# Attention, a gated feed-forward and a maxout feed-forward: which engine makes the low parts of the value weights

## The chip, the cores and the metric

The kernel runs on one core of a Trainium2 chip. The metric is device time in microseconds (us) of one execution, taken as the median over several runs. Five engines work side by side, each on its own instruction queue and in the order of that queue: PE (TensorE, matrix products), DVE (VectorE, elementwise work), ACT (ScalarE, activations and copies), POOL (GpSimd, elementwise work here), and SP (SyncE), which only issues DMAs. A wait between engines is a semaphore.

## The reference, cut to what matters

```python
scores = q @ k.T / sqrt(D)                 # B=4, H=8, S=576, D=64
# heads 0-3: local window of 32; heads 4-7: same position modulo 32; both causal
attn = softmax(where(mask, scores, -1e9))
x = (attn @ v) reshaped to 2304 x 512
g = x @ w_gate;  val = x @ w_val           # 512 x 1536 each
x = (silu(g) * val) @ w_out                # 1536 x 512
h = max(x @ w1, x @ w2, x @ w3)            # 512 x 768 each
return h @ w_out2                          # 768 x 512
```

The weights come in as 64-bit floats.

## The kernel before

Each matrix product in the feed-forwards is made from split numbers: an operand is a high part (rounded to the format `F32R`) and a low part (what the rounding left), and one product is three matmuls, high by high, high by low and low by high (`product`, lines 484 to 486). So every weight tile goes through these steps before PE can use it:

- `load` (L138) brings the 64-bit words of a 128x512 tile into SBUF by a DMA of SP.
- `convert` (L141 to L159) makes a 32-bit float from the two halves of each word: two ACT instructions (L151, L152), then four on DVE (L154, L156, L157, L158). The first three tiles have a step or two on POOL instead.
- `split_w` (L161 to L170) makes the high part by an ACT copy (L126), the low part by one subtraction, weight minus high part (L129), on the engine that `step_split` hands over. Value and output weights are then stored to DRAM by a DMA of SP (L170), since later columns of tokens read them back (`reload`, L723). Gate weights stay in SBUF.

There are 36 such tiles in the first feed-forward: a gate tile g, a value tile v and an output tile o for each of the 12 slices f of its inner dimension. Their order (L686 to L691) is g0, v0, g1, v1, o0, g2, v2, o1 and so on to g11, v11, o10, o11. `step_split` counts them in `n_split`; for each third one, from the first, it takes DVE for the low part, and POOL for the others. By the order above the DVE ones are g0 and v1 to v11, twelve in all; v0, the other gate tiles and all output tiles are POOL's.

The 2304 tokens stand in five columns c = 0 to 4 of some 480 tokens. Attention for column 0 comes first. Then loops run over c and, within it, over f: `emit_gate` (12 matmuls into ps_g, then Silu by ACT, L504), `emit_val` (12 matmuls into ps_v, then DVE multiplies by the gate, L511, ACT makes the high part hh, L126, and POOL the low part hl, L129), and one slice late `emit_out` (12 matmuls into ps_y). While c is 0, a `weight_step` stands ahead of the gate, the value and the end of each slice: it loads a tile, converts one and splits one. Attention of the next column is put between (`attention_steps`): block softmax on DVE, ACT and POOL (L294 to L304), its results split by ACT and DVE (L328, L329), and, for rows that aren't done on PE, elementwise products on POOL (L397, L419) that DVE sums (L400, L422). From column 1 on no weights of the first feed-forward are converted any more, but those of the second are, at a slower pace. After column 4 the second feed-forward runs.

The order in which each engine gets its instructions is not the order of the source: a planner lays them out when the kernel is built, by an estimate of when each would be ready. From then on each engine's queue is fixed.

Of the kernel before, what the change touches and what calls it, by code (L numbers as in the profile page):

```python
# [57 lines left out]
def tile_attention_swiglu_maxout(  # L58
# [11 lines left out]
    nc = tc.nc  # L70
# [29 lines left out]
    def f32(ap):  # L100
        return ap.bitcast(F32)
# [20 lines left out]
    def split(hi, lo, src, hi_eng, lo_eng):  # L122
        if hi_eng is nc.gpsimd:
            a = nc.gpsimd.tensor_scalar(hi, src, 1.0, 1.0, ALU.mult, ALU.mult)
        elif hi_eng is nc.scalar:
            a = nc.scalar.activation(hi, src, AF.Copy)  # L126
        else:
            a = nc.vector.tensor_copy(hi, src)
        return a.ins, lo_eng.tensor_tensor(lo, src, f32(hi), ALU.subtract).ins  # L129
# [31 lines left out]
    def split_w(key, lo_eng):  # L161
        name = f"{key[0]}{key[1]}"
        if key[0] == "g":
            wt[key] = tuple(wpool.tile([128, 512], F32R, name=f"w{p}_{name}", tag="w") for p in "hl")
        else:
            t = (wv_p if key[0] == "v" else wo_p).tile([128, 2, 512], F32R, name=f"w_{name}", tag="w")
            wt[key] = (t[:, 0], t[:, 1])
        split(*wt[key], cvt.pop(key), nc.scalar, lo_eng)
        if key[0] != "g":
            nc.sync.dma_start(wdr[key], f32(t))  # L170
# [515 lines left out]
    first = [("g", 0), ("v", 0)]  # L686
# [5 lines left out]
    n_load, n_cvt, n_split = [0], [0], [0]  # L692
# [17 lines left out]
    def step_split(eng):  # L710
        if n_split[0] < limit[0]:
            key = order[n_split[0]]
            split_w(key, nc.vector if n_split[0] < len(first) and n_split[0] % 3 == 0 else eng)
            n_split[0] += 1

    def weight_step():
        step_load(n_cvt[0] + AHEAD)
        step_cvt()
        step_split(nc.gpsimd)
# [6 lines left out]
    if True:  # L726
# [8 lines left out]
        for i in range(len(blocks) + lag):  # L735
# [5 lines left out]
            if i >= lag:  # L741
                blocks[i - lag].transpose(nc.vector if i % 3 == 2 else nc.scalar)
                blocks[i - lag].pv()
        step_split(nc.gpsimd)
        step_split(nc.gpsimd)
        step_load(n_cvt[0] + 2)
        step_cvt()
# [178 lines left out]
```

## Time and profile before

| | |
|---|---|
| median of 3 runs | 881.88 us (879.77 to 882.62) |
| the profiled execution's own time | 881.39 us |
| span of its instructions | 879.6 us |
| busy share of the span: PE, DVE, ACT, POOL | 93%, 63%, 44%, 43% |
| column 0 of the first feed-forward | from about 42 us to about 190 us |

The busy share is an average over stages. A DVE instruction that stands on its engine counts as busy also while it is held up, so busy time has to be laid beside what the same instruction takes at its shortest. In the views below, a start time is in us from the beginning of the span, the number after it is the duration, and "[0.92 <-DVE w_v L129]" says that the engine was idle for 0.92 us until that instruction of another engine ended.

### The profile page before, as it was taken

The page shows a single profiled execution, that of the slowest core. Times are in us where ns is not written, and L with a number is a line of the kernel's source. Part 1 is how long each engine was busy: PE and PEld are TensorE (multiplying, and loading weights), DVE is VectorE, ACT ScalarE, POOL GpSimd, SP SyncE. Part 2 cuts the span into 40 slices and gives each one's busy share as a digit, 9 for nine tenths or more (in the row PEclk, how much of TensorE's full clock was granted, in tenths as well). Part 3 has the DMA queues.
Part 4 walks back from the last instruction along what each step waited for, and adds up shares of the span by engine and source line. Part 5 has one row for each costly group of instructions (what it writes and reads, how often), then busy time and mean ns, then how long its engine had stood idle before and what let it go on. Part 6 is the DMA issues. An engine that isn't in the chain of part 4 may idle for free.

```text
span 879.6 us, 12559 instructions
## 1 busy us (share of the span) xinstructions
PE 820.3 (93%) x4376; PEld 731.7 (83%) x4376; DVE 555.9 (63%) x1097; ACT 384.0 (44%) x857; POOL 382.3 (43%) x301
## 2 busy tenths in 40 slices
PE   5789879898999989999998889999999999999997
PEld 5677658687788878999897779989999899989986
DVE  2988999967757598668768943433545254433441
ACT  4778586734445454364634233432335123422221
POOL 0443654474757676667596632430213021211110
PEclk9789789999999999999999989999999999999999
DMA  9868757896695759869676687578856476453601
GB/s 234 244 219 289 235 187 260 320 366 189 209 330 192 245 190 312 275 207 319 208 249 234 224 268 225 189 245 342 330 217 213 182 251 245 175 215 118 241 1 72
DMA packets 81774, 203.76 MB, mean 232 GB/s; under 512 B 9484, under 2 KB 50224, under 8 KB 78128
## 3 DMA queue, kind: packets, MB, share of 16 engines
q1 hardware_dynamic: 81712, 202.97, 68.1%
q8 instruction: 35, 0.57, 0.2%
q14 instruction: 27, 0.22, 0.1%
HBM read 161.26 MB, written 41.68 MB: 231 GB/s over the span
## 4 chain that ended last, share of the span: by engine, by line
PE 49%; DVE 10%; DMA 4%; ACT 4%; issue 3%; POOL 2%; SPq 0%; DVEq 0%; ACTq 0%; POOLq 0%
PE ps_a L585 13%; PE ps_z L658 8%; PE ps_c L585 6%; PE ps_b L585 3%; PE ps_v L484 2%; PE ps_g L484 2%; PE ps_v L485 2%; PE ps_v L486 2%; PE ps_g L486 2%; PE ps_g L485 2%; PE ps_y L484 2%; PE ps_y L486 2%; PE ps_y L485 2%; DVE w L156 2%; DMA w_v<-wvdr 1%
## 5 line engine op out<-in xcount | busy, mean ns | idle before, releaser
L129 POOL TENSOR_TENSOR hl<-t,hh 128x384 fp32r<-128x384 f32 x36 | 37.6, 1048 | 208.5 <-ACT hh L126 167.2
L484 PE MATMUL ps_g<-xh,wh_g 128*128 128x448 f32 (+1 forms) x240 | 94.4, 393 | 10.4 <-ACT ht L504 8.1
L129 POOL TENSOR_TENSOR hl<-ht,hh 128x448 fp32r<-128x448 f32 (+1 forms) x60 | 75.5, 1258 | 60.5 <-ACT hh L126 58.8
L419 POOL TENSOR_TENSOR pr<-stv,stsc 128x1088 f32<-128x1088 f32 (+17 forms) x44 | 75.2, 1710 | 58.1 <-DVE sto L422 35.9
L486 PE MATMUL ps_v<-xh,w_v 128*128 128x448 f32 (+1 forms) x240 | 91.5, 381 | 8.2 <-DVE w_v L129 8.2
L484 PE MATMUL ps_v<-xh,w_v 128*128 128x448 f32 (+1 forms) x240 | 92.4, 385 | 4.4 <-ACT w_v L126 2.4
L585 PE MATMUL ps_a<-yhT,wr 128*128 128x384 f32 x324 | 94.4, 338 | 0.6 <-ACT s L599 0.6
L486 PE MATMUL ps_g<-xh,wl_g 128*128 128x448 f32 (+1 forms) x240 | 92.7, 386 | 1.3 <-POOL wl_g L129 1.3
L485 PE MATMUL ps_g<-xl,wh_g 128*128 128x448 f32 (+1 forms) x240 | 92.4, 385 | 0.0
L485 PE MATMUL ps_v<-xl,w_v 128*128 128x448 f32 (+1 forms) x240 | 91.1, 379 | 0.0
L485 PE MATMUL ps_y<-hl,w_o 128*128 128x448 f32 (+1 forms) x240 | 89.2, 376 | 1.0 <-POOL hl L129 1.0
L397 POOL TENSOR_TENSOR pr<-stk,stq 128x1088 f32<-128x1088 f32 (+17 forms) x44 | 76.9, 1747 | 30.1 <-DVE stsc L400 23.2
L486 PE MATMUL ps_y<-hh,w_o 128*128 128x448 f32 (+1 forms) x240 | 86.4, 377 | 2.3 <-POOL w_o L129 2.3
L484 PE MATMUL ps_y<-hh,w_o 128*128 128x448 f32 (+1 forms) x240 | 86.2, 380 | 0.2 <-ACT w_o L126 0.2
L599 ACT ACTIVATE s<-ps_a 128x384 f32<-128x384 f32 x81 | 39.4, 490 | 98.4 <-PE ps_a L585 98.1
L126 ACT ACTIVATE hh<-ht 128x448 fp32r<-128x448 f32 (+1 forms) x60 | 35.2, 587 | 106.0 <-DVE ht L511 105.6
L658 PE MATMUL ps_z<-wo2t,hh 128*128 128x512 f32 x216 | 64.8, 392 | 0.9 <-ACT osb L667 0.7
L484 PEld LDWEIGHTS ps_g<-xh,wh_g 128*128 128x128 f32 x240 | 47.2, 197 | 19.1 <-ACT ht L504 10.5
L511 DVE TENSOR_TENSOR ht<-ps_v,ht 128x448 f32<-128x448 f32 (+1 forms) x60 | 37.8, 630 | 37.9 <-PE ps_v L486 26.6
L585 PEld LDWEIGHTS ps_a<-yhT,wr 128*128 128x128 f32 x324 | 59.7, 188 | 1.7 <-ACT s L599 1.1
L486 PEld LDWEIGHTS ps_v<-xh,w_v 128*128 128x128 f32 x240 | 46.1, 192 | 15.1 <-DVE w_v L129 10.3
L484 PEld LDWEIGHTS ps_v<-xh,w_v 128*128 128x128 f32 x240 | 46.2, 192 | 11.1 <-DVE ht L511 3.4
(134 smaller groups left out, 1971.5 us busy)
## 6 DMA issues: line engine op xcount, KB each, us to landing
wr<-wsdr SPq DMA_DIRECT2D x27, 1792.0 KB, 7.2
raw<-in_w_dram SPq DMA_DIRECT2D x60, 512.0 KB, 4.8
w_v<-wvdr SPq DMA_DIRECT2D x48, 512.0 KB, 5.0
w_o<-wodr SPq DMA_DIRECT2D x48, 512.0 KB, 4.9
wsdr<-whi SPq DMA_DIRECT2D x27, 256.0 KB, 3.3
wvdr<-w_v SPq DMA_DIRECT2D x12, 512.0 KB, 4.1
wodr<-w_o SPq DMA_DIRECT2D x12, 512.0 KB, 5.2
loct<-in_loc_dram SPq DMA_DIRECT2D x24, 192.0 KB, 6.5
```

Source lines behind the costliest of these rows:

```text
L126: a = nc.scalar.activation(hi, src, AF.Copy)
L129: return a.ins, lo_eng.tensor_tensor(lo, src, f32(hi), ALU.subtract).ins
L156: nc.vector.tensor_scalar(w, w, 3, 0x3FFFFFFF, ALU.logical_shift_left, ALU.bitwise_and)
L397: eng.tensor_tensor(pv, self.k[:, 0:i + 1, :], self.q[:, r:r + 1, :].to_broadcast([128, i + 1, D]), ALU.mult)
L419: eng.tensor_tensor(pv, self.v[:, :, 0:i + 1], self.sc[:, r:r + 1, 0:i + 1].to_broadcast([128, D, i + 1]), ALU.mult)
L484: nc.tensor.matmul(ps, wh, xh, start=first, stop=False)
L485: nc.tensor.matmul(ps, wh, xl, start=False, stop=False)
L486: nc.tensor.matmul(ps, wl, xh, start=False, stop=last)
L511: m = nc.vector.tensor_tensor(t, ps[:, :n], t, ALU.mult).ins
L585: nc.tensor.matmul(ps, wts[:, c, a, ks], y[k][b], start=first and k == q == 0, stop=k == 1 and q == 2, skip_group_check=True,)
L599: nc.scalar.activation(s, self.a, AF.Copy)
L658: nc.tensor.matmul(z[j], a[:, ts], w[:, f, b], start=f == q == 0, stop=f == NF2 - 1 and q == 2)
```

## The change

In `step_split` the low part of every tile is made by the engine handed over, which is POOL at each call. The twelve low parts g0 and v1 to v11 leave DVE for POOL. What is computed, its buffers and its DMAs are the same.

```diff
     def step_split(eng):
         if n_split[0] < limit[0]:
             key = order[n_split[0]]
-            split_w(key, nc.vector if n_split[0] < len(first) and n_split[0] % 3 == 0 else eng)
+            split_w(key, eng)
             n_split[0] += 1
```

## Rows read from the trace of the kernel before

**Rows 1.** The page, first part: busy time and share of each engine.
```profile
PE 820.3 (93%) x4376; PEld 731.7 (83%) x4376; DVE 555.9 (63%) x1097; ACT 384.0 (44%) x857; POOL 382.3 (43%) x301
```
**Rows 2.** Busy us by stretch: length, PE, PEld, DVE, ACT, POOL, clock, DMA, GB/s.
```profile
50.00:90.00 40.00, 36.77 (x188) 29.83 (x188) 36.60 (x72) 31.44 (x61) 17.04 (x12) 0.96 0.82 269
90.00:178.00 88.00, 73.75 (x372) 59.26 (x373) 87.67 (x156) 59.74 (x127) 47.29 (x33) 0.88 0.75 252
178.00:200.00 22.00, 20.53 (x103) 17.39 (x102) 14.80 (x32) 7.78 (x23) 16.43 (x9) 1.00 0.99 355
```
**Rows 3.** DVE groups, 26 to 185 us: count, busy us, mean ns, idle before, releaser.
```profile
L158 DVE CUSTOM_DVE_ANT_0 w<-w,q 128x1024 uint16<-128x1024 uint16 x36 | 34.4, 960 | 0.1
L129 DVE TENSOR_TENSOR w_v<-w,w_v 128x512 fp32r<-128x512 f32 x11 | 11.0, 996 | 2.6 <-ACT w_v L126 2.6
```
**Rows 4.** By tile or line: shortest, median and longest ns of one.
```profile
L129 DVE TENSOR_TENSOR w_v<-w,w_v x11: 676/682/2559, 45.4 to 174.6; 128x512 fp32r<-128x512 f32 x11
L129 POOL TENSOR_TENSOR wl_g<-w,wh_g x11: 1282/1306/1794, 45.7 to 167.5; 128x512 fp32r<-128x512 f32 x11
L158 DVE CUSTOM_DVE_ANT_0 w<-w,q x36: 670/682/1776, 31.1 to 177.5; 128x1024 uint16<-128x1024 uint16 x36
L511 DVE TENSOR_TENSOR ht<-ps_v,ht x12: 640/646/659, 52.1 to 179.3; 128x480 f32<-128x480 f32 x12
```
**Rows 5.** Timeline: POOL low parts, each with the DVE instruction beside it.
```profile
53.63 1.80 POOL L129 TENSOR_TENSOR w_o<-w,w_o 128x512 fp32r<-128x512 f32 x1 [4.94 <-ACT w_o L126]
54.22 1.77 DVE L158 CUSTOM_DVE_ANT_0 w<-w,q 128x1024 uint16<-128x1024 uint16 x1
...
65.11 1.34 POOL L129 TENSOR_TENSOR w_o<-w,w_o 128x512 fp32r<-128x512 f32 x1 [1.29 <-ACT w_o L126]
65.23 1.78 DVE L158 CUSTOM_DVE_ANT_0 w<-w,q 128x1024 uint16<-128x1024 uint16 x1
...
134.25 1.31 POOL L129 TENSOR_TENSOR wl_g<-w,wh_g 128x512 fp32r<-128x512 f32 x1 [0.17 <-ACT wh_g L126]
134.28 1.33 DVE L422 TENSOR_REDUCE sto<-pr 128x64 f32<-128x1152 f32 x1
...
175.41 1.36 POOL L129 TENSOR_TENSOR w_o<-w,w_o 128x512 fp32r<-128x512 f32 x1 [1.62 <-ACT w_o L126]
175.82 1.49 DVE L157 SCALAR_TENSOR_TENSOR w<-raw,w 128x512 int32<-128x512 int32 x1
```
**Rows 6.** A POOL group, 26 to 185 us, columns as in rows 3.
```profile
L129 POOL TENSOR_TENSOR wl_g<-w,wh_g 128x512 fp32r<-128x512 f32 x11 | 16.0, 1452 | 12.2 <-ACT wh_g L126 10.8 <-issue 1.4
```
**Rows 7.** PE's waits, 50 to 178 us: total, times, longest.
```profile
PE ps_v L486 <- DVE w_v L129: 8.2, 6, 2.9
PE ps_y L486 <- POOL w_o L129: 2.3, 1, 2.3
```
**Rows 8.** Timeline around the low part of v7.
```profile
121.77 0.62 ACT L126 ACTIVATE w_v<-w 128x512 fp32r<-128x512 f32 x1
126.95 2.66 DVE L156 TENSOR_SCALAR w<-w 128x512 int32<-128x512 int32 x1
129.52 0.68 DVE L129 TENSOR_TENSOR w_v<-w,w_v 128x512 fp32r<-128x512 f32 x1
130.26 0.73 PE L486 MATMUL ps_v<-xh,w_v 128*128 128x480 f32 x1 [2.93 <-DVE w_v L129]
```
**Rows 9.** Timeline at the end of the conversions and behind it.
```profile
174.59 0.68 DVE L129 TENSOR_TENSOR w_v<-w,w_v 128x512 fp32r<-128x512 f32 x1
175.32 0.49 PE L486 MATMUL ps_v<-xh,w_v 128*128 128x480 f32 x1 [0.92 <-DVE w_v L129]
179.05 0.39 DVE L329 TENSOR_TENSOR xl<-ps_a,xh 128x120 fp32r<-128x120 f32 x1
181.31 0.37 PE L486 MATMUL ps_g<-xh,wl_g 128*128 128x480 f32 x1
201.72 0.86 PE L309 MATMUL ps_a<-cst,sm 128*96 128x128 f32 x4 [2.38 <-POOL sm L304]
```

## The prediction

> **What bounds the kernel now.** The page's first part [rows 1] seems to settle it: PE is busy for 93% of the span, DVE for 63%, POOL for 43%. That is an average, and eleven of the twelve low parts start between 45.4 and 174.6 us [rows 4], so the second view is busy time by stretch [rows 2]. From 90 to 178 us DVE is busy 87.67 of 88 us, while PE is busy 73.75 and its clock was granted at 0.88, a mean of the two levels of 2.4 and 1.2 GHz. POOL is busy 47.29. Before that, from 50 to 90 us, DVE is busy 36.60 of 40. So while column 0 runs, DVE sets the pace with the conversions, PE waits for weights, and POOL has room. Behind 178 us DVE is at 14.80 of 22 and PE goes on.
>
> The third view says what DVE is busy with [rows 3, 4]. L158 takes 682 ns at the median, 670 at the shortest, but 960 on average and 1776 at the longest: it is held up. The timeline names by whom [rows 5]: at 65.11 POOL starts a low part that takes 1.34 us, L158 starts at 65.23 and ends some 0.55 us behind POOL's end, having taken 1.78. The hold is 1.78 - 0.68 = 1.09 us. It isn't so for all kinds: L511, which reads PSUM, takes 640 to 659 ns in all twelve cases [rows 4], and the sum L422, which reads one SBUF tensor, runs to its 1.33 us beside a POOL low part as if alone [rows 5]. The conversion steps and the low parts themselves are of the kind that is held.
>
> The fourth view is PE's waits in this stretch [rows 7]: the longest in total is on the DVE low parts, 8.2 us in 6 waits, as DVE reaches them late. For v7 ACT has made the high part at 122.39, and DVE does the low part at 129.52, behind an L156 that took 2.66 us beside a long POOL product [rows 8]; PE waited 2.93.
>
> **Removed from DVE.** Twelve subtractions, each 0.68 us at the median [rows 4], from an engine that is full: 12 x 0.68 = 8.2 us. Their mean of 996 ns [rows 3] is larger by holds; I don't count those as gain, since the next held kind in the queue takes the hold. DVE also idled 2.6 us ahead of eleven of them, for ACT's high part [rows 3]. I take 2.0 of it, as it counts only where what stands behind is ready.
>
> **Added to POOL.** Twelve subtractions of 1452 ns mean [rows 6], 1282 at the shortest [rows 4]: 17.4 us. POOL has 88 - 47.29 = 40.7 us free between 90 and 178 alone [rows 2], so their time as such is hidden. On POOL's queue hl, w_o's low parts, the softmax products L304 and the products L397 and L419 may stand behind them, each later by up to 1.5 us. hl has a slice of cover, as the output product comes one slice late. For w_o the cover has been gone once: 2.3 us of PE wait [rows 7]; once more would cost as much. SP stores a value tile when its low part is there, so the store, and the raw loads queued behind it, follow the low part; where that comes sooner, so do they. g0 is the first tile, before column 0's matmuls begin at about 42 us, and counts in the sums for DVE alone.
>
> **What twelve more POOL low parts cost DVE** is the price that decides, and no row shows it for v tiles in this place. I went through the 32 POOL low parts between 53 and 177 us (11 w_o, 11 hl, 10 wl_g), the first and last of which stand in rows 5, and took what the DVE instruction beside each lost against its shortest: 27.3 us, 0.85 each. The ends: the ten wl_g give 0.52, as some meet sums and PSUM readers; a full hold is 1.09 [rows 5]. A v low part will stand on POOL directly behind wl_g or hl, while DVE has conversions queued, so I take the mean: 12 x 0.85 = 10.2 us. DVE's sum is then 10.2 - 8.2 = +2.0, and with the idle time 10.2 - 8.2 - 2.0 = 0. Below nothing is in reach: 12 x 0.52 - 10.2 = -4.0. Above: 12 x 1.09 - 8.2 = +4.9.
>
> Rows 5 show a hold of 1.09 us from an operation of 1.34, and none on a sum or a PSUM reader. The Trainium skill, SBUF — State Buffer, section SBUF: two separate sides, speaks against this change: DVE and GpSimd share one pair of ports as an exclusive lock, held for a whole instruction, and a DVE instruction with two SBUF inputs, or in a mode of two ports, fully blocks behind GpSimd. The trace agrees in who is held, but not for the whole of POOL's recorded time; by the rule each move would cost the mean of 1.45 us, 12 x 1.45 - 8.2 = +9.2 us, an estimate; by the rows it is +2.0 before the idle time.
>
> **What PE makes of it.** The low part on POOL can start when ACT's high part and POOL's own queue allow, not 7 us later as for v7 [rows 8]. But PE is fed by the conversions, so its waits can't all turn into time. At the end of the stage PE waits 0.92 us for v11 at 175.32; the next thing from DVE is the last piece of column 1's input, xl, written 179.05 to 179.44 and read from 181.31 on [rows 9], so PE can run ahead there by 181.31 - 179.44 = 1.9 us before it meets the next limit. I take half of it, 1.0 us, as DVE's own order may shift.
>
> **The sum.** DVE 0, PE's lead -1.0: 881.39 - 1.0 = 880.4 us against the profiled execution (span 879.6 and 1.8 around it). That lies 0.5 below the median of the runs, 881.88; on the median's footing the forecast is 880.9. It is no change that can be measured: 0.3% of this kernel is 2.6 us, about what a measurement here can tell from none, so the bounds are 879.2 and 884.5.
>
> **Rivals.**
> Faster: the moved parts meet the cheap neighbours, as wl_g does. DVE's sum is -4.0, PE's lead the whole 1.9: -5.9 us, 876.0. For it speak PE's 8.2 us of waits [rows 7] and the clock of 0.88 [rows 2], which gives back time when waits go; against it that DVE, not PE, is full, and that behind the stage PE waits 2.38 us at 201.72 for a softmax product of POOL [rows 9], where a lead can be lost again.
> Slower: DVE meets a full hold each time, since POOL's operations now stand back to back (wl_g, v, hl) and each ends a turn in which DVE gets one instruction through. +4.9, no idle time won and no lead: 886.8. For it: the longest L158 [rows 4], and that DVE's queue between 90 and 178 us is mostly conversions. Against it: 0.85 on average includes such pairs already. It decides from 0.68 + (2.0 + 1.0 + 2.6) / 12 = 1.15 us per move if idle time and lead are won, from 0.90 if neither is.
> Nothing arrives: the low part has to queue on POOL behind hl, wl_g and the long products, and comes no sooner than from DVE. Then DVE's +2.0 stays alone: 883.9, still within the bounds. That the change doesn't act can't be: it only names another engine.
> The planner may also lay out other queues anew. What that moves isn't in the trace; I bound it on both sides by the mean of the six PE waits, 8.2 / 6 = 1.4 us.
>
> **How the numbers follow.** The forecast and the nothing-arrives case, both no change: 0.38. Faster: 0.33. Slower: 0.29, of which 0.05 for a hold as long as POOL's whole operation, 1.45 each [rows 6], 881.4 + 9.2 = 890.6. The range goes from 876.0 - 1.4 = 874.6 to 886.8 + 1.4 = 888.2, cut to 887.5, as both at their worst is unlikely.
>
> **What would show it.** In the changed trace DVE has no low part of a weight, POOL has 36. The mean of L154 to L158 rises: if the holds come to 0.85 each, their sum by some 10 us; if to 0.5, by 6; if to 1.1, by 13. PE's wait on DVE for v low parts is gone; what stands in its place (ACT's high parts, or POOL's low parts) tells whether lag or supply was the limit. The low part of v11 stands at 174.59 now [rows 9], and DVE's last conversions just behind it; they should end within 2 us of where they do. The prediction is wrong if that moves by more, or if PE's clock in this stretch rises clearly above 0.88.

## The result, and the profile after

The changed kernel is slower: 887.74 us median of 4 runs (886.65 to 888.91) against 880.90 (879.77 to 882.62) for the kernel before on the same chip. The ratio is 1.0077, 95% interval 1.0058 to 1.0096: +6.8 us, and just outside the range that was forecast (874.6 to 887.5). The profiled execution took 888.02 us, its span is 886.2.

The page's first part of the changed kernel says almost the same as [rows 1]: DVE has twelve instructions less and is busy 2 us longer, POOL twelve more and 14.5 us longer.

```profile
PE 819.2 (92%) x4376; PEld 727.5 (82%) x4376; DVE 558.0 (63%) x1085; ACT 384.1 (43%) x857; POOL 396.8 (45%) x313
```

Busy time by stretch of the changed kernel, columns as in [rows 2]: length, PE, PEld, DVE, ACT, POOL, clock, DMA share, GB/s.

```profile
50.00:90.00 40.00, 36.02 (x206) 28.50 (x205) 38.15 (x68) 31.34 (x63) 21.90 (x17) 0.96 0.76 247
90.00:178.00 88.00, 68.65 (x340) 53.84 (x339) 83.95 (x148) 58.20 (x122) 50.20 (x37) 0.90 0.73 240
```

From 90 to 178 us DVE is no longer full: 83.95 of 88 us, where it was 87.67. PE did less there, 68.65 us and 340 matmuls, where it was 73.75 and 372. So DVE was relieved in the stage that it had bounded, and the stage got longer all the same.

The groups of DVE's conversion steps, 26 to 185 us, and POOL's new one (columns as in [rows 3]), then the same POOL group as shortest, median and longest:

```profile
L158 DVE CUSTOM_DVE_ANT_0 w<-w,q 128x1024 uint16<-128x1024 uint16 x36 | 35.5, 987 | 0.2
L157 DVE SCALAR_TENSOR_TENSOR w<-raw,w 128x512 int32<-128x512 int32 x36 | 34.4, 957 | 0.3
L156 DVE TENSOR_SCALAR w<-w 128x512 int32<-128x512 int32 x36 | 26.0, 724 | 0.3
L154 DVE TENSOR_SCALAR w<-w 128x512 f32<-128x512 f32 x33 | 22.1, 668 | 5.0 <-ACT w L152 5.0
...
L129 POOL TENSOR_TENSOR w_v<-w,w_v 128x512 fp32r<-128x512 f32 x12 | 17.1, 1423 | 15.1 <-ACT w_v L126 13.7 <-issue 1.3
...
L129 POOL TENSOR_TENSOR w_v<-w,w_v x12: 1275/1454/1592, 36.6 to 174.5; 128x512 fp32r<-128x512 f32 x12
```

Before, L158 took 34.4 us [rows 3] and the other three:

```profile
L157 DVE SCALAR_TENSOR_TENSOR w<-raw,w 128x512 int32<-128x512 int32 x36 | 32.8, 917 | 0.1
L156 DVE TENSOR_SCALAR w<-w 128x512 int32<-128x512 int32 x36 | 21.7, 604 | 0.2
L154 DVE TENSOR_SCALAR w<-w 128x512 f32<-128x512 f32 x33 | 21.3, 646 | 1.2 <-ACT w L152 1.2
```

So the four conversion groups took 110.2 us together before; now 118.0. That is +7.8, or 0.65 for each of twelve new POOL operations. L154 waited 1.2 us for ACT's L152 before and waits 5.0 now: part of DVE's new room is a wait for another engine.

PE's waits of the changed kernel from 50 to 185 us (total, times, longest), and the longest of them in the timeline:

```profile
PE ps_g L484 <- ACT wh_g L126: 8.9, 4, 6.2
PE ps_v L484 <- DVE ht L511: 2.7, 2, 1.7
...
PE ps_v L486 <- POOL w_v L129: 1.3, 2, 0.8
...
127.45 0.77 PE L484 MATMUL ps_g<-xh,wh_g 128*128 128x480 f32 x1 [6.16 <-ACT wh_g L126]
```

The wait that the change is aimed at is nearly gone: 8.2 us on DVE's low parts [rows 7], 1.3 on POOL's. In its place PE waits 8.9 us for high parts of gate tiles (0.9 before), and one wait alone is 6.16. It is for the eighth gate tile, g7, and this is what stood around it on POOL, DVE and ACT:

```profile
120.15 2.46 POOL L419 TENSOR_TENSOR pr<-stv,stsc 128x1152 f32<-128x1152 f32 x1
120.61 2.28 DVE L154 TENSOR_SCALAR w<-w 128x512 f32<-128x512 f32 x1 [0.70 <-ACT w L152]
...
126.77 0.63 ACT L126 ACTIVATE wh_g<-w 128x512 fp32r<-128x512 f32 x1 [1.38 <-DVE w L158]
```

An L154 of that tile stood beside a long POOL product for 2.28 us, and ACT could make the high part only at 126.77. In the kernel before, ACT had started it at 118.55. The last conversion ends late too; here it is with PE's first gate matmul of column 1, in the changed kernel:

```profile
182.16 1.40 DVE L158 CUSTOM_DVE_ANT_0 w<-w,q 128x1024 uint16<-128x1024 uint16 x1
...
184.91 0.38 PE L484 MATMUL ps_g<-xh,wh_g 128*128 128x480 f32 x1
```

And the same three, g7's high part, the last conversion and the gate matmul, in the kernel before:

```profile
118.55 0.62 ACT L126 ACTIVATE wh_g<-w 128x512 fp32r<-128x512 f32 x1
...
177.52 0.69 DVE L158 CUSTOM_DVE_ANT_0 w<-w,q 128x1024 uint16<-128x1024 uint16 x1
...
179.36 0.37 PE L484 MATMUL ps_g<-xh,wh_g 128*128 128x480 f32 x1
```

The last conversion ends at 183.56, where it ended at 178.21 before, and PE's gate matmul starts at 184.91, where it was 179.36. So +5.4 us is there when column 0 ends, of the 6.6 by which the two profiled executions differ (888.02 - 881.39).

Two things changed at once: twelve operations went to another engine, and the planner, given other costs, laid out all queues anew. The experiments take them apart.

### The profile page after: what moved, and what is told of

It is laid out like the page before. It is cut to its first block, busy times and chain, and to the rows that moved or that the text cites. A ratio compares the mean times of both kernels' runs of the same rounds, so it can differ in the third digit from the quotient of the medians.

```text
span 886.2 us, 12557 instructions
## 1 busy us (share of the span) xinstructions
PE 819.2 (92%) x4376; PEld 727.5 (82%) x4376; DVE 558.0 (63%) x1085; ACT 384.1 (43%) x857; POOL 396.8 (45%) x313
## 4 chain that ended last, share of the span: by engine, by line
PE 45%; DVE 13%; issue 4%; DMA 3%; ACT 3%; POOL 3%; SPq 0%; DVEq 0%; ACTq 0%; POOLq 0%
PE ps_a L585 12%; PE ps_z L658 8%; PE ps_c L585 6%; PE ps_b L585 3%; DVE w L156 2%; PE ps_g L484 2%; PE ps_v L484 2%; PE ps_g L485 2%; PE ps_y L486 2%; PE ps_y L485 2%; PE ps_g L486 2%; PE ps_y L484 2%; PE ps_v L486 2%; PE ps_v L485 2%; DMA w_v<-wvdr 1%
## 5 line engine op out<-in xcount | busy, mean ns | idle before, releaser
L486 PE MATMUL ps_g<-xh,wl_g 128*128 128x448 f32 (+1 forms) x240 | 92.9, 387 | 2.2 <-POOL wl_g L129 2.2
L486 PE MATMUL ps_v<-xh,w_v 128*128 128x448 f32 (+1 forms) x240 | 90.9, 379 | 1.3 <-POOL w_v L129 1.3
L486 PE MATMUL ps_y<-hh,w_o 128*128 128x448 f32 (+1 forms) x240 | 87.2, 374 | 1.0 <-POOL w_o L129 1.0
L484 PEld LDWEIGHTS ps_g<-xh,wh_g 128*128 128x128 f32 x240 | 47.0, 196 | 29.0 <-ACT ht L504 12.2
L484 PEld LDWEIGHTS ps_v<-xh,w_v 128*128 128x128 f32 x240 | 46.0, 192 | 19.4 <-DVE ht L511 7.9
L158 DVE CUSTOM_DVE_ANT_0 w<-w,q 128x1024 uint16<-128x1024 uint16 x60 | 54.8, 914 | 0.8
```

The costliest lines, as they stand in the source:

```text
L158: nc.vector.tensor_tensor(w, w, q, ALU.add)
L484: nc.tensor.matmul(ps, wh, xh, start=first, stop=False)
L486: nc.tensor.matmul(ps, wl, xh, start=False, stop=last)
```

## The experiments

**How an order is held.** In most of the kernels below the planner's list of one variant is read out, and another variant is built with it: each engine's instructions get, one after the other, an edge of order without a semaphore. So one kernel has the queues of another, and only what is named differs. The core of it, where `plan` is the other variant's list and `traced` this one's instructions as they were written:

```python
for n in plan:
    i = traced[n]
    if i.engine in last:
        tc.add_manual_dep(
            i, last[i.engine].name,
            _mybir.DependencyInfo(_mybir.DependencyClass.NoSync, _mybir.DependencyReason.DATA),
            reason="plan",
        )
    last[i.engine] = i
```

Each result is given against the kernel before on the same chip. The theory at the start: the time comes from twelve more holds on DVE. The rivals: the new order; low parts that come too late from POOL's queue.

**The move alone, and the order alone.** The first has the order of before with the twelve low parts on POOL, the second the order of the changed kernel with them on DVE. `MOVED` lists which of the twelve go to POOL: `program` takes that list, `plan` is read out of a first build, and the second build, held to it, is the kernel that runs.

```diff
-            split_w(key, nc.vector if n_split[0] < len(first) and n_split[0] % 3 == 0 else eng)
+            split_w(key, eng if n_split[0] % 3 or n_split[0] // 3 in MOVED else nc.vector)
...
+    _, _, plan = program([])
+    nc, arrays, _ = program(range(12), plan)
...
+    _, _, plan = program(range(12))
+    nc, arrays, _ = program([], plan)
```

> The planner laid out the queues of the changed kernel anew: about 560 lines of difference on PE alone. Here every engine's queue has the order of the kernel before, instruction by instruction; only the twelve low parts go to POOL, each into POOL's queue at the place in the planner's list where DVE had it. So this is the move of the engine without the new order. Theory H (holds): twelve POOL operations hold DVE for more than the 8.2 us that they save; then this kernel has the whole loss, 886 to 890 us, and DVE is as full between 90 and 178 us as before. Theory O (order): the move alone is about even (8.2 us removed, 12 holds of 0.71 us as the changed trace shows, 8.5 us), and the loss comes from the new order of the queues; then 879 to 883 us, the time of the kernel before.

Measured: 884.38 us, ratio 1.0035 [1.0016, 1.0054], +3.1 to +3.7 (by ratio and by medians).

> The other half: every queue in the order of the changed kernel, but the twelve low parts on DVE, each in DVE's queue at the place in the planner's list where POOL had it. Theory H: without the twelve holds the time is that of the kernel before, 879 to 883 us. Theory O: the order alone brings the loss, 886 to 890 us, and PE's long wait for a gate weight of some 6 us near 127 us stays. If both halves lose 3 to 4 us, both theories hold in part.

Measured: 883.74 us, ratio 1.0036 [1.0021, 1.0052], +3.1. So by the medians each is about half of the +6.8, and they add. The profiled executions don't have these shares: that of the move alone took 882.54 us, 1.8 below its median, and that of the order alone 887.44, the longest of its twelve. They show what waits for what, not how much of the time each half is. The long wait of some 6 us belongs to the order: PE's waits from 50 to 178 us in the kernel with the order alone show it with the low parts on DVE.

```profile
PE ps_g L484 <- ACT wh_g L126: 8.3, 4, 6.2
...
PE ps_v L486 <- DVE w_v L129: 2.1, 2, 1.5
```

Even the wait on DVE's low parts has shrunk there, 8.2 to 2.1 us, with no low part moved: the new order did that, and not POOL.

**Is it the place in POOL's queue, or v11?** In the first of these two each moved low part stands on POOL directly behind its high part in the list, in the second v11's low part stays on DVE; else they are the move alone.

```diff
+    for high, low in SPLITS:
+        if low in [x[1] for x in SPLITS[0::3]]:
+            plan.remove(low)
+            plan.insert(plan.index(high) + 1, low)
...
+    nc, arrays, _ = program(range(11), plan)
```

> As the run of the move alone (queues in the order of the kernel before, the twelve low parts on POOL, +3 us), but each low part stands in POOL's queue at the place in the planner's list directly behind its high part, not where DVE had it. Theory H (holds): the number of holds is the same, so the time is that of the move alone, 883 to 886 us. Theory Q (place in POOL's queue): in the move alone PE waited 7.5 us in 4 waits for these low parts, 3.5 of it for v11 at the end behind a long product; placed early these go, and the time is 879 to 882 us.

Measured: 884.21 us, 1.0036 [1.0020, 1.0052].

> As the run of the move alone, but v11, the last value tile, keeps its low part on DVE; eleven move. In the move alone PE waited 3.5 us for v11's low part at 176.9 us, where the kernel before waited 0.9. Theory Q (place in POOL's queue, at the end of the stage): with v11 back, most of the +3 us goes, 880 to 882 us. Theory H: eleven of twelve holds stay, 883 to 886 us.

Measured: 883.88 us, 1.0031 [1.0017, 1.0046]. Both are the move alone again, within their intervals. Neither the place in POOL's queue nor v11 at the end of the stage is its cause.

**Work removed, holds added.** The move takes work from DVE and adds operations on POOL. The next two do one each, in the order of before. In the first, nobody makes the low parts of v1 to v11 (they are not computed) and a DMA fills their place; in the second, DVE keeps its low parts and POOL does twelve subtractions into a spare tile.

```diff
+        if MOVED and lo_eng is nc.vector and key != ("g", 0):
+            hi = nc.scalar.activation(wt[key][0], cvt.pop(key), AF.Copy)
+            SPLITS.append((hi.ins, nc.sync.dma_start(f32(wt[key][1]), wdr["v", 0][:, 1]).ins))
...
+        lo = split(*wt[key], cvt.pop(key), nc.scalar, lo_eng)[1]
+        if MOVED and lo_eng is nc.vector:
+            EXTRA.append((lo, nc.gpsimd.tensor_tensor(spare[0], f32(wt[key][0]), f32(wt[key][0]), ALU.subtract).ins))
```

> The first half of the move alone, in the order of the kernel before: the low parts of v1 to v11 leave DVE, and POOL doesn't make them either. A DMA fills their place with the low part of v0 (so they aren't computed; g0 stays as it was); its 256 KB stand in SP's queue directly ahead of the high part. DVE loses 11 x 0.68 = 7.5 us of work and gets no new hold. Theory W (DVE's work is all on the path, as my sum had it): 873 to 875 us. Theory V (much of it lay where DVE would else wait for ACT): 2 to 4 us less than before, 877 to 879 us.

Measured: 878.37 us, 0.9974 [0.9956, 0.9992], -2.3 by the ratio (-1.9 by medians): much less than the 7.5 us of work that is gone.

> The second half alone, in the order of the kernel before: DVE makes all its low parts as before, and POOL makes twelve more operations of the same size (high part minus high part, into a spare tile that nobody reads), each at the place in POOL's queue that the moved low part had. Twelve more holds, no work removed. Theory W: the move costs +3.5 in all and gave back 8.2 of work, so the holds alone are +11 to +12: 891 to 893 us. Theory V: the holds alone are +6 to +7: 886 to 888 us. The two halves should add up to the move alone, +3.5.

Measured: 887.57 us, 1.0075 [1.0054, 1.0096], +6.6 by the ratio (+7.3 by medians): 0.55 us for each operation. The sum of the two, +4.3, is near the move's +3.1 to +3.7, and that looked like an answer. But PE's waits of the first kernel, the one with the DMA filler, say otherwise (its lines from L169 on are four higher, L490 is L486 of before):

```profile
PE ps_v L490 <- DMA w_v<-wvdr: 7.5, 5, 2.2
```

PE waited 7.5 us for the filler. The experiment had put a late transfer in the place of the late low part, so its -2.3 is no price of removed work. Three further kernels make it clean: column 0's matmuls use v's high part a second time in the place of the low part of v1 to v11, so that PE needs no low part. In the first, no low part of v1 to v11 is made, and the high part is stored twice, in halves. In the second POOL makes the low parts, in the third DVE, for the stores alone.

```diff
+        if MOVED and lo_eng is nc.vector and key != ("g", 0):
+            wt[key] = (t[:, 0], t[:, 0])
+            hi = nc.scalar.activation(wt[key][0], cvt.pop(key), AF.Copy)
+            SPLITS.append((hi.ins, nc.sync.dma_start(wdr[key][:, 1], f32(t[:, 0])).ins))
+            nc.sync.dma_start(wdr[key][:, 0], f32(t[:, 0]))
...
         split(*wt[key], cvt.pop(key), nc.scalar, lo_eng)
+        if MOVED and ("v", 1) <= key <= ("v", NF):
+            wt[key] = (t[:, 0], t[:, 0])
```

> The low parts of v1 to v11 are made by nobody: PE multiplies with the high part in both places, SP stores the high part twice (two halves for one whole), and every queue keeps the order of before. What is left out is the value weights' low parts, eleven subtractions of DVE, with no filler that PE could wait for, as the run with the DMA filler had (PE waited 7.5 us for it). Work counts in full: DVE loses 11 x 0.68 = 7.5 us and 2.6 us of idle time, the conversions end 7 to 10 us sooner, 871 to 873.5 us. Work removed is worth only the 2.3 us that the run with the filler gave, since DVE then waits for ACT (1.2 us before, 4.9 there): 877.5 to 879. In between, 874 to 877: the filler's lateness had hidden a part of the gain.

Measured: 874.69 us, 0.9935 [0.9915, 0.9955], -6.0 by medians. In this kernel the last L158 ends early:

```profile
169.73 1.49 DVE L158 CUSTOM_DVE_ANT_0 w<-w,q 128x1024 uint16<-128x1024 uint16 x1
```

It ends at 171.22, 7.0 us sooner than before. Busy time from 26 us to the end of the last conversion (columns as in [rows 2]), of the kernel before, of this one and of the move alone:

```profile
26.00:178.20 152.20, 129.48 (x724) 105.05 (x723) 146.22 (x303) 109.87 (x253) 77.00 (x54) 0.89 0.76 251
```

```profile
26.00:171.21 145.21, 125.75 (x728) 102.35 (x729) 135.76 (x291) 109.35 (x252) 78.66 (x54) 0.93 0.77 257
```

```profile
26.00:179.66 153.66, 126.48 (x716) 101.48 (x713) 144.94 (x288) 109.33 (x251) 94.36 (x65) 0.90 0.74 247
```

Without v's low parts DVE is busy 10.5 us less, and idle 3.5 us more (9.45 for 5.98). In the move alone it is busy 1.3 us less and idle 2.7 more, and the last conversion ends 1.5 later. Nearly all of the idle time lies ahead of 90 us. DVE's longest waits from 26 to 90 us, of the kernel before and then of the one without v's low parts (its lines from L169 on are six higher, L308 is L302):

```profile
DVE w_v L129 <- ACT w_v L126: 2.6, 3, 1.4
DVE w L154 <- ACT w L152: 1.2, 2, 1.0
DVE stat L302 <- ACT sm L299: 0.5, 1, 0.5
```

```profile
DVE w L154 <- ACT w L152: 4.5, 4, 1.7
DVE stat L308 <- ACT sm L305: 2.4, 2, 2.0
```

The wait ahead of the low parts is gone, and other steps wait for ACT instead. Behind the conversions PE loses a little again, on POOL's softmax products (from 178 to 300 us, where it was 3.6 before):

```profile
PE ps_a L315 <- POOL sm L310: 4.5, 3, 2.3
```

> The order of before, GpSimd makes the twelve low parts, but in column 0 PE multiplies with the high part in the place of the low part of v1 to v11, which only the stores read (left out are those eleven products with the low parts). Holds 6.6 and work removed -5.9 as measured one by one: +0.7, about 881.5. If the move alone (+3.1 to +3.7) is only these two and they don't add, it stays at 883.5 to 884.5; if the rest of it is PE's wait for a low part that comes no sooner from GpSimd, this run is 2 to 3 us below the move alone.

Measured: 885.03 us against 881.68, 1.0041 [1.0023, 1.0059], +3.4.

> The order and the engines of before, DVE makes the twelve low parts, but in column 0 PE multiplies with the high part in the place of the low part of v1 to v11, which only the stores read (left out are those eleven products with the low parts). PE has no wait on DVE's low parts (8.2 us before), DVE has all its work. If these waits are the price: up to 8 us less, 873 to 876. If they only stand for DVE being behind, another wait takes their place: within 1.5 us of before, 879.5 to 882.

Measured: 880.00 us against 881.68, 0.9981 [0.9962, 1.0001], -1.7, and no change that can be told. These two were the most telling runs. PE's waits on v's low parts can be taken away whole, and the time hardly moves: with the parts on POOL not at all (+3.4, as the move alone), with them on DVE by 1.7 of 8.2 us. So the wait in [rows 7] was not the price; it showed that DVE was behind. And the difference of the first and the second prices POOL's twelve operations: PE waits for no low part of v1 to v11 in either, and POOL makes twelve in one of them. It is 3.4 + 6.0 = 9.4 us, 0.78 each, and by the two intervals some 2.4 us either way. Small differences are left in it: g0's low part is on DVE in the first, and its stores go in halves. Their conversion groups, 26 to 185 us, first without and then with POOL's twelve:

```profile
L158 DVE CUSTOM_DVE_ANT_0 w<-w,q 128x1024 uint16<-128x1024 uint16 x36 | 36.6, 1021 | 0.1
L157 DVE SCALAR_TENSOR_TENSOR w<-raw,w 128x512 int32<-128x512 int32 x36 | 30.8, 862 | 0.2
L154 DVE TENSOR_SCALAR w<-w 128x512 f32<-128x512 f32 x33 | 23.3, 706 | 4.5 <-ACT w L152 4.5
L156 DVE TENSOR_SCALAR w<-w 128x512 int32<-128x512 int32 x36 | 20.4, 570 | 0.2
```

```profile
L158 DVE CUSTOM_DVE_ANT_0 w<-w,q 128x1024 uint16<-128x1024 uint16 x36 | 37.0, 1031 | 0.1
L157 DVE SCALAR_TENSOR_TENSOR w<-raw,w 128x512 int32<-128x512 int32 x36 | 32.2, 902 | 0.2
L156 DVE TENSOR_SCALAR w<-w 128x512 int32<-128x512 int32 x36 | 25.5, 711 | 0.2
L154 DVE TENSOR_SCALAR w<-w 128x512 f32<-128x512 f32 x33 | 25.1, 760 | 4.7 <-ACT w L152 4.7
```

111.1 and 119.8: +8.7 us of holds on the conversions, next to 9.4 us of time. The same operations cost 6.6 (4.8 to 8.5) when DVE still makes its low parts. The intervals of the two prices overlap, so whether they differ at all is open.

**The other way.** If POOL's operations cost DVE more than DVE's own would, the low parts that POOL already makes belong on DVE. The three kernels are all 36 on DVE in the order of before; the same, in the planner's own order; and the first with column 0's hl on DVE too. In the first and third `MOVED` is a list of one number in the build that runs, and only switches the edit on.

```diff
+            split_w(key, nc.vector if len(MOVED) == 1 or n_split[0] % 3 == 0 else eng)
...
+            split_w(key, nc.vector)
...
+        last_val[:] = [m, *split(hh, hl, t, nc.scalar, nc.vector if MOVED and c == 0 else nc.gpsimd)]
```

> The order of the kernel before in every queue, and all 36 low parts of the first feed-forward's weights on DVE: the 24 that POOL had (11 gate tiles, v0, 12 output tiles) move the other way. Theory H: if a POOL low part holds DVE for 0.85 us and takes 0.68 on DVE, 24 x (0.68 - 0.85) = -4 us, so 876 to 879 us. Theory O: holds and work cancel, and the late place in DVE's queue costs PE some waits, so 880 to 885 us. DVE's L154 to L158 should have shorter means than before in either case.

Measured: 877.04 us, 0.9954 [0.9938, 0.9969], -3.6.

> All 36 low parts of the first feed-forward's weights on DVE, with queues that the planner lays out for this anew. With the order of the kernel before, the same gave 877.0 us, 3.6 less than before. If the order is neutral, 875 to 879 us. If a new order costs as it did in the changed kernel (3.2 us), 879 to 883 us; it can also gain.

Measured: 876.93 us, 0.9950 [0.9932, 0.9968].

> As the run with all 36 low parts on DVE in the order of the kernel before (877.0 us), and the twelve low parts hl of column 0's gated products on DVE, too. Theory H: an hl on POOL held DVE for 0.93 us in the kernel before, and the same on DVE takes about 0.65; 12 x (0.65 - 0.93) = -3.4, so 873 to 875 us. Against it: DVE reaches hl late and PE waits for it at the output product; then 877 to 881 us.

Measured: 876.26 us, 0.9944 [0.9925, 0.9963]. Twenty-four more operations on an engine that was busy for 87.67 of 88 us made the kernel faster. The stretch and two groups of the first kernel:

```profile
90.00:178.00 88.00, 74.12 (x383) 60.06 (x382) 87.46 (x175) 59.35 (x125) 30.52 (x19) 0.90 0.79 265
...
L158 DVE CUSTOM_DVE_ANT_0 w<-w,q 128x1024 uint16<-128x1024 uint16 x36 | 27.9, 779 | 0.1
L156 DVE TENSOR_SCALAR w<-w 128x512 int32<-128x512 int32 x36 | 18.4, 515 | 0.2
```

DVE is as full as before, with 175 instructions in place of 156; L158 has fallen from 960 ns to 779. Taking hl as well gave 0.8 us beyond, which the intervals can't tell from nothing; the 873 to 875 us expected did not come, and why is not settled.

**What an order is worth.** Two kernels move one low part each and let the planner lay out all queues: v11's alone, and the first tile's (g0) alone. Set beside the kernel before, DVE's queue differs in some 550 lines in the one and 610 in the other. A last one holds the order of the first of them and puts all 36 low parts on DVE.

```diff
+            split_w(key, eng if n_split[0] % 3 or n_split[0] == 3 * 11 else nc.vector)
...
+            split_w(key, eng if n_split[0] % 3 or n_split[0] == 3 * 0 else nc.vector)
...
+    _, _, plan = program([11])
+    nc, arrays, _ = program([0], plan)
```

> One low part of the twelve moves, that of v11, and the planner lays out the queues for it: 546 lines of difference on DVE's queue against the kernel before, 496 on PE's. The move itself should cost a twelfth of 3.5 us, 0.3. If a new order is neutral, 880 to 882 us; if new orders scatter as that of the changed kernel did (+3.2), it is more than 2 us off to one side.

Measured: 876.35 us against 880.31, 0.9949 [0.9931, 0.9967], -4.0.

> The same with another single move, that of g0's low part: 614 lines of difference on DVE's queue, 504 on PE's. The move itself should cost 0.3 us or less. If a new order is neutral, 880 to 882 us; if orders scatter, more than 2 us off to one side, not the same one as for v11.

Measured: 883.84 us, 1.0035 [1.0020, 1.0049], +3.1 by the ratio and +3.5 by medians.

> Two gains put together: every queue in the order that the planner laid out when v11's low part alone moved (that kernel gave 876.35 us, 4.4 less than before), and all 36 low parts on DVE (in the order of the kernel before this gave 3.6 less). If order and holds are separate prices, they add up: 872 to 874 us. If the gain of that order lay in v11's own move, or both gains are the same waits, 876 to 877 us.

Measured: 871.34 us against 881.28, 0.9891 [0.9861, 0.9921], -9.9: faster than both kernels of this case. The order's -4.0 and the -3.6 of all low parts on DVE add: -7.6 lies in the interval of this -9.9 (-12.2 to -7.0). The busy time from 178 to 300 us, of the kernel before, of the one with v11's order alone and of this one:

```profile
178.00:300.00 122.00, 115.91 (x628) 97.26 (x628) 83.45 (x181) 58.30 (x130) 80.99 (x65) 0.99 0.75 255
```

```profile
178.00:300.00 122.00, 120.81 (x664) 103.02 (x663) 88.71 (x188) 64.39 (x137) 82.66 (x67) 1.00 0.81 266
```

```profile
178.00:300.00 122.00, 120.81 (x671) 103.50 (x669) 90.42 (x188) 63.95 (x136) 81.82 (x65) 1.00 0.80 267
```

PE's waits in that stretch, of the kernel before and then of the one with v11's order alone:

```profile
PE ps_a L309 <- POOL sm L304: 3.6, 3, 2.4
PE ps_g L484 <- ACT ht L504: 1.1, 1, 1.1
```

```profile
PE ps_g L484 <- ACT ht L504: 1.2, 1, 1.2
```

The good order does its work in column 1, behind the stage of the tile that was moved: PE's waits on the softmax products L304 are gone, and PE is busy 120.81 of 122 us.

## Why the prediction was wrong

**Bound and holds: right, the size within wide bounds.** DVE's conversions set column 0's pace, and POOL's operations hold them. The price of a move's POOL side was put at 0.85 us, 10.2 for twelve; measured 9.4 give or take 2.4 without v's low parts on DVE, 0.78 each, and 6.6 (4.8 to 8.5) with them. The Trainium skill, SBUF — State Buffer, section SBUF: two separate sides, has the one that loses the shared ports blocked for the whole instruction. In the three held pairs of [rows 5] DVE ends 0.54 to 0.56 us behind POOL's end, as an instruction of 0.68 us would that was held until about then, so the trace agrees with that sentence better than the prediction says. The estimate of 1.45 for each operation needs a conversion that stands ready at each operation's start, and the mean did not come near it. Twelve full holds of 1.09, the slower rival, did not come either. That its 886.8 us lies next to the measured 887.7 is luck, since half of the loss is the order.

**Work removed and idle time: the step that failed.** They were put at 8.2 and 2.0 us in full. Eleven of the twelve parts were worth 6.0 us where those terms give 11 x 0.68 + 2.0 = 9.5. It wasn't that the holds came back: the low parts' group is 11.0 us long [rows 3], and without it the conversions took 111.1 us where they took 110.2, so DVE's busy time fell by 10.5 us, more than was counted. What failed is that idle time can be won on top of work. DVE was full from 90 us on, but only 36.60 of 40 us busy from 50 to 90 [rows 2], and there ACT was the next limit: its idle time was to fall by 2.0 us and rose by 3.5. So the conversions ended 7.0 us sooner. Behind them PE's waits on POOL's softmax products L304 rose from 3.6 to 4.5 us, which is about what is missing from there to the 6.0. The work itself was sized a little too large. The low part of v11 starts at 174.59 and takes 0.68 [rows 9], but the next instruction of DVE starts 0.60 behind it:

```profile
175.19 0.41 DVE L156 TENSOR_SCALAR w<-w 128x512 int32<-128x512 int32 x1
```

The move alone, in its profiled execution, shows the same in two parts. Two conversions of the kernel before, and the same two there:

```profile
92.42 1.64 DVE L158 CUSTOM_DVE_ANT_0 w<-w,q 128x1024 uint16<-128x1024 uint16 x1
...
177.52 0.69 DVE L158 CUSTOM_DVE_ANT_0 w<-w,q 128x1024 uint16<-128x1024 uint16 x1
```

```profile
92.26 1.63 DVE L158 CUSTOM_DVE_ANT_0 w<-w,q 128x1024 uint16<-128x1024 uint16 x1
...
178.97 0.69 DVE L158 CUSTOM_DVE_ANT_0 w<-w,q 128x1024 uint16<-128x1024 uint16 x1
```

The conversion that ends at 94.06 us in the kernel before ends at 93.89 there: up to that point the move gave next to nothing. The last one ends 1.5 us later than before: behind that point, where DVE is full and seven of the parts lie, each cost some 0.23 us. How the medians come to +3.1 to +3.7 from there is not shown by any trace.

**PE's lead: not there.** It was put at 1.0 us. Taking PE's waits on v's low parts away altogether gave 0 with the parts on POOL and 1.7 on DVE. The prediction's remark that PE is fed by the conversions was right and should have set this term at nothing; the rival "nothing arrives" was the better reading.

**The planner's order: the bound was too small.** It was put at 1.4 us on either side, the mean of six PE waits. Measured +3.1 for the changed kernel's order, and -4.0 and +3.5 for the two single moves. A mean wait says nothing about what hundreds of moved places can do; a single wait that came of it is 6.16 us.

**The sum** by measured terms: 881.4 - 6.0 + 9.4 + 3.1 = 887.9, where the profiled execution took 888.0. The first two terms together are by their making the +3.4 of the kernel whose moved parts PE doesn't read, so what the sum tests is that the move and the order add. Predicted were -10.2, +10.2, -1.0 and an order of 0. So the direction was missed by two terms of about 4 us (removed work with its idle time) and 3 (the order), and by a lead of 1.0 that did not come.

**The signs named.** No wait of PE on DVE low parts and 36 low parts on POOL came as said; the conversions' sum rose by 7.8, between the 6 and the 10 named; the clock stayed, 0.90 for 0.88. The last conversions were to end within 2 us, and moved by 5.4: by its own sign the prediction is wrong. The move alone moves them by 1.5, so this sign caught the order.

The prediction had the sign in its hand. By its own working a low part on POOL holds DVE for 0.85 us, and DVE does one in 0.68 [rows 4]: while DVE is full, it loses more by the move than it gives away, as the move alone showed behind 94 us. The +2.0 that this made was turned to -1.0 by idle time and a lead, and of both the trace showed only that they stood there, not that they would turn into time. A POOL low part of a v tile takes 1454 ns at the median and DVE's took 682. The Trainium skill, GPSIMD Engine Reference, section 4.1 Engine selection, puts elementwise work on VectorE and not on GPSIMD, as some 2 times slower there with two inputs. The trace has 2.1 times, and the kernel with all 36 on DVE agrees, -3.6 us.

## What to carry to other kernels

Before moving work from a full engine to a free one, ask what the operation costs the full engine when the other does it, and where that exceeds the full engine's own time, move work the other way: here 24 low parts brought to the full engine gave 3.6 us. Ask also, stretch by stretch, whether the engine is full: where it isn't, work taken from it comes back in part as waits for other engines, here 3.5 of 10.5 us. A wait that grows long behind a bound engine shows that the engine is late: take the wait away by feeding something else, and see if the time moves, before you count it as gain. With a planner, replay the old order under the edit first; a new order alone moved this kernel by some -4 to +3 us, as much as the edits did.

## What the runs showed of the hardware

An engine at 87.67 of 88 us busy could take 24 more operations of 0.68 us, 16 us in all, and the kernel became 3.6 us faster, as its other instructions got shorter: L156 went from 604 ns on average to 515 and L158 from 960 to 779. A busy share tells that an engine is occupied, not that it is working. The held time is counted as busy by the profile, and shows when an instruction is laid beside the shortest of its shape [rows 4]. Twelve subtractions on POOL cost the conversions of DVE 8.7 us and the kernel 9.4 in one pair of kernels, though neither DVE nor PE reads what eleven of them made.
